# Row tiles of 32 in the tap matmuls, a filter sum by accumulating transfers, and a new order of work in a fused convolution and feed-forward kernel

## The chip, the cores and the metric

The kernel runs on one core of one Trainium2 chip. The metric is the device time of one launch in microseconds (us), as a median over runs. A profiled execution gives, beside it, a trace of every instruction on the five engines: PE (matmul), DVE (vector), ACT (scalar), POOL (GpSimd) and SP (which only issues transfers). Weight loads of the PE have a row of their own, PEld.

## The reference

The block is a gated long convolution followed by a feed-forward part, on 2048 tokens of width 640, all in bf16.

```
def reference(...):                       # S, D, F = 2048, 640, 1728
    x = A_q
    q = layernorm(x)
    k_shift = sum over t = 0..3 of  k delayed by (3-t) tokens * shift_k[:, 3-t]      # four taps per channel
    kv = k_shift * v
    y = irfft(rfft(kv, 2S) * rfft(ssm_k, 2S))[:S]  (bf16)  +  kv * ssm_D             # causal convolution over all tokens
    h = x + q * y
    n = layernorm(h)
    return h + (silu(n @ w_gate) * (n @ w_up)) @ w_down
```

## The kernel before

The 2048 tokens are cut into four blocks of 512, numbered 0 to 3. Within a block the tokens lie four to a partition (token 4p+j on partition p), so a tile of 512 x 640 is [128 partitions, 4, 640]. The convolution is done by odd-frequency transforms of length 512 per block: a filter spectrum for each of the four pieces of the filter (`kfwd`, tasks `kf0` to `kf3`), a signal spectrum for each block (`xfwd`, `xf0` to `xf3`), products of them on DVE (`prod(j, i)`, tasks `pji`, signal block j into output block i), and an inverse transform (`inverse`, tasks `ivi.j`, one for each of four token tiles of 128). After the inverse come the gating, the second layer norm and a transposing transfer into `hnT` (`hti.j`), and then the feed-forward part of that block (`ffn`): gate and up matmuls `fg` and `fu` in two halves of 256 tokens (a name such as `fg1.02` is block 1, half 0, third group), silu and copy out of PSUM on ACT (`sg`, `su`, `sv`), their product on DVE (`mu`), and the down matmuls `dn` (with `rs` for the residual sum, `ra` for an accumulating transfer of it into the token tile, and `out` for the store).

The filter spectra are combined (`kcomb`) so that C[m] holds the sum of the spectra m-1 and m: C[1] by two DVE additions (tasks `kc1.s0`, `kc1.s2`), C[2] by one DVE addition of 128 x 5120 elements (`kc2.s`, L687), C[3] by two accumulating transfers from POOL's queue (`kc3.0`, `kc3.1`; the lists `KS` and `KD` say which).

The taps (`taps`, tasks `tpi.c`) are matmuls. For a channel block c of 128 channels the four tap weights lie as diagonal matrices in `diag`; a matmul takes 64 channels (the rows), 128 columns of the shifted, transposed k as weights, and up to four diagonal pieces of 64 columns as the moving side. Seven shifts s = 0, 1, 2, 3, -1, -2, -3 need 4, 3, 2, 1, 3, 2, 1 such pieces. The two halves of 64 channels are two row tiles of the array and write to the two PSUM banks of one PSUM unit. A block has five channel blocks, taken as three tasks: `tpi.0` (two channel blocks), `tpi.2` (two), `tpi.4` (one); 70 matmuls in all. For blocks 1 to 3 (`KVACT`) an evacuation `ke` copies each task's result to SBUF, and DVE multiplies it with v (`kv`, L745). Block 0 multiplies straight from PSUM.

Nothing is scheduled at run time. `_Graph` records tasks with what they read and write; `PLAN` then lists by number, for each engine, the order of its tasks, and for each PSUM tile which of four units (two banks each) it lives in. Engines run their list strictly in order, and wait with semaphores where a task of another engine must be done. So a matmul task whose unit has not been evacuated stops the PE, whatever stands behind it. `fills` puts a few dummy matmuls before two of the first tasks.

The lines of the profile that matter below: L584, L602 and L622 are matmuls of the transforms, L734 the taps, L922 and L927 the inverse, L1032 gate and up, L1118 and L995 down; L458, L460 and L461 are evacuations (ACT, and DVE's two forms), L780 the products on DVE, L571 every accumulating transfer, L840 a small power on POOL in the layer norms, L453 the transposing transfers.

Of the kernel before, what the change touches and what calls it, by code (L numbers as in the profile page):

```python
# [50 lines left out]
class _Graph:  # L51
# [41 lines left out]
    def add(self, name, engs, fn, kind, r=(), w=(), pr=(), pw=(), skip=(), dma=False):  # L93
# [4 lines left out]
        t.opens = None  # L98
# [18 lines left out]
        for pt in pw:  # L117
            if not pt.writers:
                t.opens = pt
            else:  # L120
                t.deps.add(pt.writers[-1])
            pt.writers.append(t)
            pt.users.append(t)
            t.tiles.append(pt)
# [10 lines left out]
    def arrange(self, plan):  # L135
# [19 lines left out]
        for t in self.order["pe"]:  # L155
            if t.opens is not None:
                prev = last.get(t.opens.unit)
                if prev is not None:
                    t.pre = {x for x in prev.users if x.eng != "pe"}
                    t.deps.update(t.pre)  # L160
                last[t.opens.unit] = t.opens
# [21 lines left out]
    def emit(self, block):  # L183
# [29 lines left out]
        for t in self.glob:  # L213
            kn = known[t.eng]
            fill = self.fills.get(t.name)
            if fill:
                wait_for(t, t.pre | {x for x in t.deps if x.name == fill[0]})
                prog["pe"].append(lambda e, t=t, fill=fill: self.filler(e, t.opens, *fill))
# [50 lines left out]
    "act":  # L269
# [10 lines left out]
    "dve":  # L280
# [948 lines left out]
```

## Time and profile before

| | before |
|---|---|
| median of 3 runs | 258.16 us (257.98 to 258.31) |
| span of the profiled execution | 256.0 us |
| what lies around the span, against the median | 2.1 us |
| PE busy | 248.5 us, 97% |
| DVE busy | 199.8 us, 78% |
| ACT busy | 184.6 us, 72% |
| POOL busy | 58.6 us, 23% |

The profiled execution's time as such is not listed; its span is, and the difference to the median is taken as constant. In the views, busy times count an instruction from its start to its end; since matmuls overlap, an engine that is busy all the time may still have issued late, and the time between the starts of two matmuls says more than the busy share. A row of the timeline merges equal instructions: start, length, engine, line, and how many.

### The profile page before, as it was taken

To read this page: it belongs to the slowest core of one execution; us is meant where nothing else is said; L and a number is where in the kernel's file an instruction comes from. 1 tells how busy PE (TensorE), PEld (TensorE's weight loads), DVE (VectorE), ACT (ScalarE), POOL (GpSimd) and SP (SyncE) were. 2 spreads that over 40 slices of the span, in tenths; PEclk is the share of its full clock that TensorE was granted. 3 is DMA by queue.
4 is the path that set the end of the run, shared out by engine and by line. 5 is a ranking of instruction groups with operands and counts; after the bars stand their busy time and mean duration, and the time that the engine had idled before them with its cause. 6 is when DMAs were issued, how large, how long until landed. Compare 5 with 4: busy or idle time off the path is not lost.

```text
span 256.0 us, 5303 instructions
## 1 busy us (share of the span) xinstructions
PE 248.5 (97%) x2253; PEld 194.7 (76%) x2253; DVE 199.8 (78%) x256; ACT 184.6 (72%) x302; POOL 58.6 (23%) x56
## 2 busy tenths in 40 slices
PE   7999997999999999999999999999999999999995
PEld 4767773587888766888887766788886678888763
DVE  3698999999999999999999989999959534111142
ACT  2489999999996895587899789739981854526410
POOL 1001003082312053950030813334130314000000
PEclk9999999999999999999999999999999999999999
DMA  6999946787995049886956036497870142600011
GB/s 224 323 339 208 403 161 134 220 207 192 326 188 95 0 75 126 150 165 168 248 100 109 3 55 139 108 213 139 149 128 0 30 100 43 140 0 3 0 45 57
DMA packets 37620, 35.29 MB, mean 138 GB/s; under 512 B 21203, under 2 KB 32478, under 8 KB 37598
## 3 DMA queue, kind: packets, MB, share of 16 engines
q1 hardware_dynamic: 31792, 23.82, 33.2%
q0 software_dynamic: 5792, 11.14, 25.3%
q8 instruction: 17, 0.28, 0.4%
q14 instruction: 5, 0.04, 0.1%
q10 hardware_dynamic: 14, 0.01, 0.0%
HBM read 16.55 MB, written 2.62 MB: 75 GB/s over the span
## 4 chain that ended last, share of the span: by engine, by line
PE 59%; DVE 32%; DMA 4%; POOL 1%; SPq 1%; issue 1%; ACT 0%; DVEq 0%
PE ps L1032 32%; PE ps L1118 16%; DVE tt L780 9%; DVE Y L780 5%; DMA tab<-cst_tab 4%; PE ps L602 3%; PE ps L922 2%; DVE gu L1053 2%; DVE C L780 2%; DVE XH L637 2%; DVE C L564 2%; PE ps L995 2%; PE ps L622 2%; PE ps L584 2%; POOL mv L840 1%; SPq L450 1%
## 5 line engine op out<-in xcount | busy, mean ns | idle before, releaser
L1118 PE MATMUL ps<-Wd,gu 128*128 128x320 bf16 (+1 forms) x420 | 58.7, 300 | 0.0
L1118 PEld LDWEIGHTS ps<-Wd,gu 128*128 128x128 bf16 (+1 forms) x420 | 38.7, 97 | 18.4 <-issue 3.6
L780 DVE TENSOR_TENSOR tt<-XH,C 128x2560 bf16<-128x2560 bf16 (+1 forms) x31 | 47.8, 1572 | 0.6 <-ACT XH L458 0.6
L1053 DVE TENSOR_TENSOR gu<-gu,ub 128x1024 bf16<-128x1024 bf16 (+1 forms) x32 | 19.9, 621 | 26.4 <-ACT gu L1040 13.8
L1040 ACT ACTIVATE gu<-ps 128x1024 bf16<-128x1024 f32 (+1 forms) x32 | 29.4, 924 | 12.1 <-PE ps L1032 11.9
L1045 ACT ACTIVATE ub<-ps 128x1024 bf16<-128x1024 f32 x24 | 24.6, 1024 | 13.3 <-PE ps L1032 11.4
L1032 PE MATMUL ps<-hnT,GB 128*128 128x256 bf16 x280 | 34.0, 273 | 0.0
L1032 PE MATMUL ps<-hnT,UB 128*128 128x256 bf16 x280 | 33.8, 273 | 0.0
L1032 PEld LDWEIGHTS ps<-hnT,UB 128*128 128x128 bf16 x280 | 27.3, 98 | 3.4 <-ACT KO L458 0.2
L1032 PEld LDWEIGHTS ps<-hnT,GB 128*128 128x128 bf16 x280 | 27.2, 98 | 3.3
L1032 PE MATMUL ps<-hnT,GA 128*128 128x256 bf16 x240 | 28.8, 273 | 0.0
L1032 PE MATMUL ps<-hnT,UA 128*128 128x256 bf16 x240 | 28.5, 273 | 0.1
L840 POOL TENSOR_TENSOR mv<-mv,half 128x1 f32<-128x1 f32 x16 | 21.2, 1328 | 23.9 <-DVE mv L838 23.9
L1032 PEld LDWEIGHTS ps<-hnT,UA 128*128 128x128 bf16 x240 | 23.4, 98 | 3.4 <-ACT C L458 0.5
L1032 PEld LDWEIGHTS ps<-hnT,GA 128*128 128x128 bf16 x240 | 23.4, 98 | 3.2 <-DVE XH L461 0.3
L843 ACT ACTIVATE qo<-xh 128x640 bf16<-128x640 bf16 x28 | 21.0, 750 | 5.8 <-DMA xh<-in_A_q_dram 3.3
L584 PE MATMUL ps<-KT,tab 128*128 128x320 bf16 x128 | 19.8, 300 | 1.8 <-ACT K3r L458 0.7
L937 ACT ACTIVATE qo<-ps,one,st 128x640 bf16<-128x640 f32 x16 | 13.7, 887 | 9.8 <-PE ps L922 9.0
L571 POOL DMA_DIRECT2D xh<-RB x12 | 10.7, 889 | 34.4 <-DVE RB L1135 23.0
L584 PEld LDWEIGHTS ps<-KT,tab 128*128 128x128 bf16 x128 | 11.4, 98 | 8.6 <-ACT K3r L458 1.6
L840 POOL TENSOR_TENSOR st<-st,half 128x4 f32<-128x4 f32 x4 | 8.0, 1988 | 33.3 <-DVE st L835 21.5
L458 ACT ACTIVATE XH<-ps 128x640 bf16<-128x640 f32 x19 | 13.3, 736 | 1.4 <-PE ps L622 0.7
(112 smaller groups left out, 384.3 us busy)
## 6 DMA issues: line engine op xcount, KB each, us to landing
C<-US POOLq DMA_DIRECT2D x6, 640.0 KB, 6.0
kc<-in_A_ssm_k_dram SPq DMA_DIRECT2D x4, 640.0 KB, 10.3
xh<-in_A_q_dram SPq DMA_DIRECT2D x4, 640.0 KB, 5.6
out_dram<-xh SPq DMA_DIRECT2D x15, 160.0 KB, 1.9
kvo<-in_A_v_dram SPq DMA_DIRECT2D x3, 640.0 KB, 4.5
xh<-RB POOLq DMA_DIRECT2D x12, 160.0 KB, 2.9
Wd<-in_B_w_down_dram SPq DMA_DIRECT2D x1, 1280.0 KB, 7.9
C<-K3r POOLq DMA_DIRECT2D x2, 640.0 KB, 8.0
```

Source lines behind the costliest of these rows:

```text
L458: return e.activation(out=dst[1], in_=src(), func=ACTF.Copy, scale=scale)
L571: return g.add(name, "pool", lambda e, n: e.dma_start(dst, src, accum_op=ALU.add, max_dma_last_dim=4096), ("acc", 2 * int(np.prod(dst.shap ...
L584: last = e.matmul(pt.f(c, W), tab[:, f, cs, j], src[:, j, c * W:(c + 1) * W], start=(j == js[0]), stop=(j == js[1]))
L780: g.add(nm, "dve", lambda e, n_: e.tensor_tensor(out=d, in0=a, in1=b, op=op), ("sb", n * D), r=[a, b], w=[d])
L840: g.add(name + "r", "pool", lambda e, n: e.tensor_tensor(out=dst, in0=tmp, in1=hf, op=ALU.pow), ("pp", 4), r=[tmp, half[:]], w=[dst])
L843: g.add(name + "m", "act", lambda e, n: e.activation(out=junk, in_=x, func=ACTF.Identity, scale=-1.0 / D, accum_out=sm), ("aa", D, 0), r=[ ...
L937: g.add(nm + "e", "act", lambda e, n, pt=pt, q2=q2, s=s, j=j: e.activation(out=q2, in_=pt.f2(W), func=ACTF.Identity, scale=s[:, 3, j:j + 1 ...
L1032: last = e.matmul(pt.f(q // 2, 256, o=256 * (q % 2)), w[:, c, f0:f0 + P], hnT[:, c, cols], start=(c == 0), stop=(c == NC5 - 1))
L1040: g.add("sg%d.%d%d" % (i, h, gp), "act", lambda e, n, pa=pa, gv=gv, nf=nf: e.activation(out=gv, in_=pa.f(0, 256 * nf).rearrange("p (f x) - ...
L1045: g.add("su%d.%d%d" % (i, h, gp), "act", lambda e, n, pb=pb: e.activation(out=ub[:].rearrange("p b x -> p (b x)"), in_=pb.f(0, 1024), func ...
L1053: g.add("mu%d.%d%d" % (i, h, gp), "dve", lambda e, n, gv=gv, ubv=ubv: e.tensor_tensor(out=gv, in0=gv, in1=ubv, op=ALU.mult), ("sb", 256 * ...
L1118: last = e.matmul(pt.f(c, W), gu[k, fb, col(i, j)], Wd[k, fb, c * W:(c + 1) * W], start=st, stop=sp)
```

## The change

Three things are changed.

1. In `taps`, blocks 1 to 3 take channel blocks 0 to 3 as one task `tpi.0` with row tiles of 32 channels: four row tiles, four PSUM banks, that is two PSUM units opened by one task. A matmul now has 32 rows and 32 to 128 columns. Channel block 4 stays a task of its own with 64-row tiles (`tpi.4`). That makes 112 + 14 = 126 matmuls a block in place of 70. There are still three evacuations of the same sizes (`kei.0a`, `kei.0b`, `kei.4`), and two products with v in place of three. Block 0 is as before.
2. `KD = (2, 3)`: C[2] is made by two accumulating transfers from POOL's queue (`kc2.1`, `kc2.0`) and not by the addition on DVE.
3. `PLAN` is another: order on every engine and PSUM units. The recorder lets one task open several PSUM tiles. An option `DV` is added and is empty.

```diff
-    KD = (3,)
+    KD = (2,3)
     DD = (2,)
+    DV = ()
...
+    T32 = ((0, 4, 32), (4, 1, 64))
...
-            for c0 in (0, 2, 4):
-                nc_ = min(2, NC5 - c0)
-                pt = g.tile()
-
-                def mm(e, n, pt=pt, c0=c0, nc_=nc_):
+            for c0, nc_, rr in T32 if i in KVACT else ((0, 2, 64), (2, 2, 64), (4, 1, 64)):
+                nr = P // rr
+                pts = [g.tile() for _ in range(nr // 2)]
+
+                def mm(e, n, pts=pts, c0=c0, nc_=nc_, rr=rr, nr=nr):
                     for b in range(nc_):
                         c = c0 + b
                         for s in (0, 1, 2, 3, -1, -2, -3):
                             j0, j1 = max(0, s), min(3, 3 + s) + 1
                             k0 = 16 + s
-                            for r in range(2):
-                                rows = slice(64 * r, 64 * r + 64)
-                                last = e.matmul(pt.f(r, 64 * (j1 - j0), o=256 * b + 64 * j0), ks[rows, c, k0:k0 + 509:4], diag[rows, c, j0 - s:j1 - s, :],
-                                                start=(s == 0), stop=(s == -3))
+                            for r in range(nr):
+                                rows = slice(rr * r, rr * r + rr)
+                                x0 = rr * r % 64
+                                last = e.matmul(pts[r // 2].f(r % 2, rr * (j1 - j0), o=4 * rr * b + rr * j0), ks[rows, c, k0:k0 + 509:4],
+                                                diag[rows, c, j0 - s:j1 - s, x0:x0 + rr], start=(s == 0), stop=(s == -3),
+                                                **({"tile_position": (rr * r, 0)} if rr < 64 else {}))
                     return last
...
+                    for h, pt in enumerate(pts):
+                        kh_ = kr[:, 2 * h:2 * h + 2]
+                        evac("ke%d.%d%s" % (i, c0, "ab"[h] if nr > 2 else ""), (kh_, kh_),
+                             lambda pt=pt, nc_=nc_, rr=rr: pt.f2(4 * rr * nc_).rearrange("p r (b y) -> p r b y", b=nc_), 8 * rr * nc_, pt)
...
             if t.opens is not None:                       # in arrange: before
-                prev = last.get(t.opens.unit)
+            for pt in t.opens:                            # after: every tile that the task opens
+                prev = last.get(pt.unit)
```

The order, by the tasks' names, at the places that matter (a `|` stands where tasks are left out):

| place | before | after |
|---|---|---|
| PE, first transforms | kt0.0 kt0.1 xf0.01 xf0.00 kf0.011 kf0.100 | kt0.0 kt0.1 xf0.00 kf0.010 kf0.011 kf0.111 |
| PE, block 1 taps | kt3.0 kf1.110 tp1.2 tp1.0 iv0.0 iv0.1 tp1.4 | kt2.1 tp1.0 kf1.000 kt2.0 tp1.4 iv0.1 iv0.0 |
| PE, between the inverse of block 0 and the first gate | kf2, kf3 and xf1: 14 tasks, then fu0.00 | kf2, kt3.0, kf3 and xf1: 18 tasks, then fg0.00 |
| PE, block 1 | dn0.3 fu1.00 fg1.00 tp2.2 tp2.0 tp2.4 fg1.02 xf2.30 | tp2.4 dn0.1 dn0.2 dn0.3 fg1.00 fu1.00 fg1.01 tp2.0 fu1.01 fg1.02 xf2.20 |
| PE, block 1 to 2 | tp3.4 tp3.0 tp3.2 fg1.13 fu1.12 dn1.1 iv2.1 iv2.0 dn1.2 iv2.3 iv2.2 dn1.3, eight xf3, fg2.00 | tp3.0 dn1.1 tp3.4 dn1.2 iv2.0 iv2.1 dn1.3, three xf3, iv2.2, five xf3, iv2.3, fg2.00 |
| evacuations of the transforms on DVE up to block 1's products | kf0e.011 (and kte0.0) | xf0e.00 kf0e.000 kf1e.000 kf2e.001 xf1e.20 xf1e.00 kte3.0 |
| POOL, after the first layer norm | iv0.0r iv0.1r kb2.1 iv0.3r iv0.2r kb3.1 kc3.1 kc3.0 | iv0.1r lp0 iv0.0r kc2.1 kb2.1 iv0.3r iv0.2r kb3.1 kc2.0 kc3.1 kc3.0 |
| SP, block 1 | ht1.0 out0.0 ht1.1 | ht1.1 ht1.0 out0.0 |

More of the change, by code (lines that the diff above doesn't have):

```diff
@@ L97, in add @@
         t.pre = set()
-        t.opens = None
+        t.opens = []
         t.tiles = []
@@ L118, in add @@
             if not pt.writers:
-                t.opens = pt
+                t.opens.append(pt)
             else:
@@ L155, in arrange @@
         for t in self.order["pe"]:
-            if t.opens is not None:
-                prev = last.get(t.opens.unit)
+            for pt in t.opens:
+                prev = last.get(pt.unit)
                 if prev is not None:
-                    t.pre = {x for x in prev.users if x.eng != "pe"}
-                    t.deps.update(t.pre)
-                last[t.opens.unit] = t.opens
+                    t.pre |= {x for x in prev.users if x.eng != "pe"}
+                last[pt.unit] = pt
+            t.deps.update(t.pre)
         for t in self.tasks:
@@ L217, in emit @@
                 wait_for(t, t.pre | {x for x in t.deps if x.name == fill[0]})
-                prog["pe"].append(lambda e, t=t, fill=fill: self.filler(e, t.opens, *fill))
+                prog["pe"].append(lambda e, t=t, fill=fill: self.filler(e, t.opens[0], *fill))
             wait_for(t, t.deps)
@@ L731, in mm @@
                             k0 = 16 + s
[L732 to L738 removed]
+                            for r in range(nr):
[4 more added lines that the diff above has]
+                                                **({"tile_position": (rr * r, 0)} if rr < 64 else {}))
+                    return last
+                g.add("tp%d.%d" % (i, c0), "pe", mm, ("tap%d" % rr, nc_), r=[diag[:, c0:c0 + nc_], ks[:, c0:c0 + nc_, :]], pw=pts)
+                pt = pts[0]
                 cols = slice(c0 * P, (c0 + nc_) * P)
@@ L799, in prod @@
                 op2(nm + ".d", yim, u[:, :, 0], u[:, :, 1], ALU.add, 4)
+                return
+            if (j, i) in DV:
+                x, k, re = XH[j % 2][:], cm[:], tt[:, 1].rearrange("p a b d -> p (a b) d")
+                im = US[:].rearrange("p a b c d -> p (a b) c d")
+                ksw = bass.AP(k.tensor, k.offset + D, [list(k.ap[0]), [2 * D, 4], [-D, 2], [1, D]])
+                nm = "p%d%d" % (j, i)
+                for f2 in range(2):
+                    s = slice(f2, f2 + 3, 2)
+                    op2(nm + ".%da" % f2, t1, x[:, s], k[:, s], ALU.mult, 4)
+                    op2(nm + ".%dc" % f2, re[:, s], t1[:, :, odd], t1[:, :, 1 - odd], ALU.subtract, 2)
+                addto(nm + ".0e", y[:, :, odd], re)
+                op2(nm + ".0b", im, x, ksw, ALU.mult, 8)
+                for q in range(2):
+                    addto(nm + ".%df" % q, y[:, :, 1 - odd], im[:, :, q])
                 return
```

27 lines of the change are left out of this document (11 added, 16 removed), and 53 rows, old and new, of the table PLAN.

## The prediction

> **What bounds the kernel now.** I read first the chain that ended last, then the busy time by stages, then the timeline of PE at the seams between the stages. The stages show how full each engine is (after the length of the stretch: busy us and instructions of PE, PEld, DVE, ACT and POOL).
>
> ```profile
> 39.80:49.20 9.40, 7.35 (x44) 3.03 (x41) 9.02 (x12) 9.40 (x18) 2.38 (x2) 1.00 0.61 129
> 49.20:113.20 64.00, 63.58 (x588) 51.34 (x588) 63.40 (x69) 53.70 (x92) 26.44 (x19) 1.00 0.74 162
> 113.20:158.50 45.30, 45.27 (x425) 36.20 (x426) 43.73 (x55) 39.42 (x68) 11.17 (x9) 1.00 0.53 113
> 158.50:161.40 2.90, 2.66 (x18) 1.27 (x17) 2.63 (x5) 2.46 (x4) 1.47 (x2) 1.00 0.51 146
> 161.40:253.40 92.00, 91.97 (x780) 74.72 (x780) 48.69 (x72) 49.33 (x81) 15.17 (x17) 1.00 0.39 78
> ```
>
> PE is full from 49.2 on, but DVE is nearly full with it up to 158.5 (63.40 of 64.00, 43.73 of 45.30). So two engines are at their bound at once: less PE work pays in full only where DVE delivers in time. The chain gives the unit prices of PE.
>
> ```profile
> 14.72 3.96 PE ps L584 x28
> 113.95 2.18 PE ps L1032 x20
> 144.67 3.88 PE ps L1118 x28
> ```
>
> 20 matmuls of 256 columns in 2.18 us are 0.426 ns a column; 28 matmuls of 320 columns take 3.8 to 3.96 us, 0.136 us each. By this price the 44 matmuls of 39.80 to 49.20 need 6.0 us of the 9.40: PE stands still for 3.4 us there. It waits for evacuations (ACT is busy 9.40 of 9.40), and has no gate matmuls to fill in with before block 0's hnT lands. The other idle times of PE after 14.72 are small; I come to two of them. The last end is PE's, plus one residual sum and a store, which stay as they are.
>
> The profiled span is 256.0 us, the median 258.16: 2.1 us lie around the span and stay. 0.2% is 0.52 us, about what a measurement of this kernel can tell from no change.
>
> **The taps.** The rows of the three tap groups:
>
> ```profile
> 138.29 2.44 PE L734 MATMUL ps<-diag,kT 64*128 64x256 bf16 x70
> 140.67 0.50 PE L1032 MATMUL ps<-hnT,GB 128*128 128x256 bf16 x3
> 32.27 2.02 PE L734 MATMUL ps<-diag,kT 64*128 64x256 bf16 x56
> 34.23 2.35 PE L927 MATMUL ps<-OS,itab 128*128 128x320 bf16 x16
> 36.51 0.65 PE L734 MATMUL ps<-diag,kT 64*128 64x256 bf16 x14
> 37.09 0.72 PE L584 MATMUL ps<-KT,tab 128*128 128x320 bf16 x4
> L734 PEld LDWEIGHTS ps<-diag,kT 64*128 64x128 bf16 x280 | 10.0, 115 | 1.1 <-issue 0.7 <-DVE kT L460 0.2
> L734 PE MATMUL ps<-diag,kT 64*128 64x64 bf16 x80 | 7.6, 194 | 0.0
> ```
>
> A block's 70 matmuls hold PE from 138.29 to 140.67, 2.38 us. One row tile streams 1024 columns a channel block (16 pieces of 64), 5120 a block, 2.18 us at 0.426; both row tiles together would be 4.36. So the two tiles run side by side already, and 0.2 us are switching. From the first start to the last is 2.44 less the last one's 0.19, so 2.25 us: 2.15 of streaming and 0.10 for everything else. Of the 35 pairs ten have only 64 columns (27 ns), so two matmuls and two weight loads fit into 27 ns. The 280 weight loads of 115 ns sum to 32 us and keep PEld busy for 10.0: three are under way at a time, so those of different row tiles don't queue up.
>
> After: four channel blocks with four tiles side by side stream 4 x 512 columns, 0.87 us; the 8 sets of four with 32 columns (14 ns) I hold at the 27 ns that the shortest pair shows, +0.11. With 0.44 for the fifth channel block and 0.07 of small costs that is 1.5 us against 2.28 (2.38 less the leaving): 0.78 saved a block, 2.34 for three. A second excursion costs what block 1's split shows: 1.96 (32.27 to 34.23) plus 0.58 (36.51 to 37.09) against 2.38, 0.16. Blocks 2 and 3 are newly split: 0.32. Net -2.0 us on PE. The bounds: -2.3 without the floor of 27 ns; if each of the 126 matmuls cost the 33 ns that 70 take now, 4.1 us a block, +5.8 in all. I take -2.0, as the pairs are nearest to it.
>
> ACT's evacuations keep number and size. A unit more is held by one task: tp1.0 to tp3.0 must find two units free. In the new order their former owners are evacuated (kf1e, su1.00 with rs0.3, su1.12 with sg1.12) while at least one other PE task runs, so I cost that at nothing; uncovered, it would be one ACT evacuation, about 1 us.
>
> **The filter sum, and what DVE gets for it.**
>
> ```profile
> L687 DVE TENSOR_TENSOR C<-C,C 128x5120 bf16<-128x5120 bf16 x1 | 2.8, 2822 | 0.0
> L461 DVE TENSOR_SCALAR KO<-ps 128x640 bf16<-128x640 f32 x1 | 0.8, 825 | 0.4 <-PE ps L584 0.4
> L745 DVE TENSOR_TENSOR kvo<-XT,kvo 128x1024 bf16<-128x1024 bf16 x6 | 3.9, 685 | 0.0
> C<-K3r POOLq DMA_DIRECT2D x2, 640.0 KB, 8.0
> 53.43 5.21 POOL L840 TENSOR_TENSOR mv<-mv,half 128x1 f32<-128x1 f32 x1
> 27.47 0.71 ACT XH L458
> 83.16 1.40 DVE tt L780
> ```
>
> DVE loses 2.82 us, and 0.15 a block where two products with v become one. But the new order gives it five evacuations more between block 0's spectrum and block 1's products (kf1e.000, kf2e.001, xf1e.20, xf1e.00, kte3.0), 5 x 0.82 = 4.1. Net it has 1.1 us more in its fullest stretch. It starts that stretch about 0.5 earlier: the last evacuation of the signal spectrum starts at 27.47 now, behind two of kt2 on ACT; in the new order these come later, and PE has 12.0 us of work from 14.72 to that spectrum's end (6 x 0.54, 7 x 1.09, kt1 1.1), so it can start at about 26.9. 0.6 is left. The two transfers take 8.0 us to land and are first read by p02.d, in the old order at 83.16, in the new behind p11; kc2.0 goes out once kb2.1 has landed and behind kb3.1, by about 68, so lands by about 77: hidden. On POOL the issues stand before iv0.3r, where a power already took 5.21 us; iv0.3n is needed for the second half's hnT only, at least two gate tasks later.
>
> **The start.** The first matmul that needs the second half of the table waits until 14.72 in either order, since SP's first ten transfers are the same.
>
> ```profile
> 13.81 0.71 PE L584 MATMUL ps<-KT,tab 128*128 128x320 bf16 x4
> 14.72 1.52 PE L584 MATMUL ps<-KT,tab 128*128 128x320 bf16 x10 [0.20 <-DMA tab<-cst_tab]
> ```
>
> Before it the old order issues xf0.01, xf0.00 and kf0.011, 20 matmuls; the new one xf0.00, kf0.010 and kf0.011, 16. Four are left for later: +0.54. The fillers now stand behind wb4, which waits for its transfer, so the taps of block 0 come about 0.6 later; that fits into the 0.9 us between 13.81 and 14.72 as far as four fewer matmuls leave room.
>
> **The stall before the gates (39.8 to 49.2).** Two queues set when the first gate can start in the new order.
>
> ```profile
> 32.68 1.49 DVE OS L564
> 37.41 1.40 DVE C L684
> 38.81 0.40 DVE xh L944
> 39.47 0.72 ACT L843 ACTIVATE qo<-xh 128x640 bf16<-128x640 bf16 x1
> 43.12 0.71 ACT L458 ACTIVATE C<-ps 128x640 bf16<-128x640 f32 x1
> 48.96 0.81 ACT L458 ACTIVATE OS<-ps 128x640 bf16<-128x640 f32 x1
> hnT<-qo SPq DMA_TRANSPOSE x16, 2.6
> ```
>
> DVE: from the butterfly yb0.0 (now 32.7, then 32.2) to iv0.0n stand five operations of 1.40, the five evacuations (4.1), four small ones of 0.40 and kv (1.6): 14.3, so 46.5, and hnT lands 2.6 later, at 49.1. ACT: it starts iv0.1e at about 36, as now, and has then to xf1e.11 twelve evacuations (0.58 apart, ten steps from 43.12 to 48.96), seven operations of the norm (0.72 to 0.87) and ke1.4: 13.2, so 49.2. The first gate comes at about 49.3, against 49.2 now, with two transforms of xf1 and two of kf3 fewer left over (1.4 us). Of this gain of 1.3 the start (+0.54) and tp1 (-0.78) explain 0.24; about 1.0 is the stall's. Half of that I give back, since kf3.110 and kf3.010 stand behind the evacuations of the first gates: -0.5. Ends: 0 and -3.4.
>
> **Block 1.**
>
> ```profile
> PE ps L622 <- DVE kvo L745: 0.4, 1, 0.4
> ```
>
> PE waits once, 0.4 us, for kv at the first xf2 (near 113), which now stands behind mu1.00; the new order puts tp2.4 four tasks ahead and two more gate tasks before the first xf2. I take this wait as gone: -0.4.
>
> **Block 1 to 2.** Here cover is lost.
>
> ```profile
> 148.53 1.26 PE L922 MATMUL ps<-Y,itab 128*128 128x320 bf16 x8
> 149.62 3.94 PE L1118 MATMUL ps<-Wd,gu 128*128 128x320 bf16 x28
> 155.56 2.56 SPq L453 DMA_TRANSPOSE hnT<-qo  x2
> 161.32 0.94 PE L1032 MATMUL ps<-hnT,GA 128*128 128x256 bf16 x7
> ```
>
> From the first inverse of block 2 (148.53) to the first gate (161.32) PE has two down tasks (7.7), four inverses (2.2) and eight xf3 (2.2), 12.1 of 12.8 us. The hnT of the first two tiles is issued until 158.1 and has landed at about 159.5: a chain of 11.0. In the new order dn1.2 comes before the inverses, so only 8.2 us of work lie there. The chain gets shorter by what DVE no longer does in its midst (an evacuation of 0.82), 10.2. PE then waits 2.0 in place of 0.7: +1.3. The bounds are +0.6 (a chain of 9.6, as for the first tile alone) and +2.1 (11.0).
>
> Block 2 to 3 has the same loss of cover, one part of a down task (8 x 0.136 = 1.1), but DVE idles there and the present order has that much in hand. 0.
>
> Sum: +0.54 -2.0 -0.5 -0.4 +1.3 = -1.06, so 258.16 - 1.06 = **257.1 us**.
>
> **Rivals.** *ACT relieved, the stall goes.* ACT is full (9.40 of 9.40) in the stretch in which PE stands still, and five of its evacuations go to DVE. If that rather than hnT sets the stretch, half of the 2.9 us that I keep goes too: 257.1 - 1.5 = 255.6. Against it: DVE is busy 9.02 of 9.40 there.
>
> *DVE late, slower.* Place: the hnT of block 1's first half. Its second transfer is issued behind a store:
>
> ```profile
> 100.20 0.36 SPq L1147 DMA_DIRECT2D out_dram<-xh  x1
> 100.61 1.21 SPq L453 DMA_TRANSPOSE hnT<-qo  x1
> 103.59 1.15 PE L1032 MATMUL ps<-hnT,UA 128*128 128x256 bf16 x9
> ```
>
> It lands at 103.2, and PE wants it at 103.59. The new order puts both transfers ahead of the store, which gives about a microsecond; DVE's 0.6 fits in. If DVE is later by over a microsecond, the first gate of block 1 waits, and what PE has saved so far is lost: block 1's taps (0.8), the 0.5 of the stall and the 0.4 at 113.2 are not gained, and 0.7 more is waited: 257.1 + 2.4 = 259.5.
>
> *The row tiles give little.* If a set of four costs two pairs (54 ns at least), the four channel blocks take 1.51, a block 2.0: 0.3 saved and not 0.78, so 257.1 + 1.4 = 258.5. If every matmul holds the array for 27 ns, the 112 take 3.05, a block 3.5, +1.2 a block: 257.1 + 2.3 + 3.7 = 263.1. Against the latter speak the pairs: 35 of them leave 0.10 us over streaming, and ten of 64 columns would need 0.27. [...]
>
> **How the numbers follow.** The forecast, 256.4 to 258.0: 0.40, of which 0.28 lie below 257.64 and 0.12 within 0.52 of 258.16. The stall goes: 0.24. DVE late: 0.28. Row tiles give little: 0.08, a quarter of it within 0.52. That makes faster 0.52, same 0.14, slower 0.34. The range leaves out the worst of the row tiles' case and the ends of the others: 255.2 (the stall mostly gone) to 259.9 (DVE a little later still).
>
> **What would show it.** L734 with 126 matmuls a block and about 1.0 us for the 112; PE at 20 matmuls of 320 columns or fewer before the wait for tab; the first L1032 at 49 to 50 with ACT full before it; no wait of L622 near 113; 2 us of idle before block 2's first gate; DVE busy as long as before. Wrong it would be if the 112 took over 1.5 us, if the first gate came before 48.5, or if L1032 waited for hnT near 104.

## The result and the profile after

| | before | after |
|---|---|---|
| median | 258.24 us (257.98 to 259.72, 4 runs) | 261.57 us (261.36 to 262.09, 4 runs) |
| ratio, 95% interval | | 1.0117 [1.008, 1.0154] |
| span of the profiled execution | 256.0 us | 259.8 us |
| PE busy, PE idle in the span | 248.5, 7.5 us | 246.6, 13.2 us |

The changed kernel is 1.2% slower, 3.3 us by the medians and 3.8 by the two profiled spans; 257.1 was forecast. PE has 1.9 us less to do, as forecast, and stands still 5.7 us longer. The busy times by stages say where (length of the stretch, then PE, PEld, DVE, ACT, POOL). The second to fourth rows run from the first gate of a block to the first gate of the next, blocks 0, 1 and 2. After:

```profile
39.80:49.20 9.40, 8.18 (x63) 5.11 (x62) 9.40 (x13) 9.40 (x19) 1.88 (x4) 1.00 0.95 257
49.67:106.42 56.75, 53.93 (x464) 42.84 (x463) 54.01 (x61) 46.56 (x82) 24.41 (x17) 1.00 0.73 141
106.42:165.11 58.69, 55.47 (x668) 43.83 (x669) 55.92 (x65) 48.19 (x79) 14.01 (x14) 1.00 0.71 131
165.11:212.22 47.11, 47.11 (x400) 38.31 (x401) 35.57 (x51) 34.19 (x60) 12.96 (x13) 1.00 0.56 110
```

The same stretches of blocks 0 and 1 before:

```profile
49.23:103.59 54.36, 54.36 (x458) 43.30 (x459) 53.76 (x59) 46.56 (x82) 18.53 (x13) 1.00 0.71 160
103.59:161.32 57.73, 57.07 (x572) 45.44 (x570) 55.90 (x70) 48.91 (x81) 20.47 (x16) 1.00 0.60 124
```

The first gate comes 0.4 later than before. Block 0's stretch is 2.4 longer, with PE's work 0.4 less; block 1's is 1.0 longer, with PE's work 1.6 less. DVE's work is the same to 0.3 us in both. Behind that nothing changes. PE's waits after (us, times, longest):

```profile
PE ps L1048 <- DMA hnT<-qo: 2.9, 2, 2.0
PE ps L943 <- ACT qo L953: 1.9, 1, 1.9
PE ps L938 <- ACT OS L454: 0.6, 1, 0.6
```

L1048 is gate and up (L1032 before). So both losses sit in front of a first gate. The chain that ended last leads into them (start, length, engine, line); first block 1's:

```profile
80.92 1.40 DVE tt L782
82.32 0.09 DVE st L854
82.49 7.56 POOL st L856
90.13 0.88 ACT qo L953
...
102.06 0.19 DVE tt L782
102.25 4.13 DMA hnT<-qo
106.42 1.59 PE ps L1048 x13
...
143.42 1.23 PE ps L731 x99
148.53 0.57 PE ps L731 x14
...
161.11 3.91 DMA hnT<-qo
165.11 0.93 PE ps L1048 x7
```

The task at 82.49 is `la1r`, a power of 128 x 4 elements on POOL, which took 1.40 us in the kernel before:

```profile
77.51 1.40 POOL L840 TENSOR_TENSOR st<-st,half 128x4 f32<-128x4 f32 x1 [1.60 <-DVE st L838]
```

ACT evacuates block 1's inverse (L953) only with its result, at 90.13 (84.89 before); PE's next inverse has no free PSUM unit meanwhile and waits 1.9, and hnT arrives 0.9 after the last down task, by a transfer that took 4.13 us (2.60 before). DVE's next instruction behind p02.a, the gate product of that inverse, waits for the same evacuation:

```profile
91.05 0.49 DVE L960 TENSOR_TENSOR xh<-xh,qo 128x640 bf16<-128x640 bf16 x1 [1.91 <-ACT qo L953]
```

So the pause of DVE in which the power ended is itself an effect of the hold: DVE had come to the first thing that needs the power's result. The chain's last rows are block 2's gate, behind a transfer of hnT of 3.91 us.

### The profile page after: what moved, and what is told of

Same layout as the page of the kernel before. It is cut to its first block, busy times and chain, and to the rows that moved or that the text cites. A ratio compares the mean times of both kernels' runs of the same rounds, so it can differ in the third digit from the quotient of the medians.

```text
span 259.8 us, 5625 instructions
## 1 busy us (share of the span) xinstructions
PE 246.6 (95%) x2421; PEld 193.7 (75%) x2421; DVE 196.8 (76%) x251; ACT 186.0 (72%) x303; POOL 59.8 (23%) x58
## 4 chain that ended last, share of the span: by engine, by line
PE 59%; DVE 26%; ACT 6%; DMA 4%; POOL 3%; issue 1%; ACTq 0%
PE ps L1048 34%; PE ps L1134 15%; DVE tt L782 8%; DVE Y L782 4%; DMA hnT<-qo 3%; POOL st L856 3%; ACT qo L953 2%; DVE C L560 2%; PE ps L731 2%; PE ps L580 2%; DVE XH L633 2%; PE ps L1011 2%; ACT qo L861 1%; PE ps L938 1%; ACT qo L859 1%; DVE gu L1069 1%
## 5 line engine op out<-in xcount | busy, mean ns | idle before, releaser
L1048 PE MATMUL ps<-hnT,UB 128*128 128x256 bf16 x280 | 34.0, 273 | 0.0
L1048 PE MATMUL ps<-hnT,GB 128*128 128x256 bf16 x280 | 34.0, 273 | 0.0
L1056 ACT ACTIVATE gu<-ps 128x1024 bf16<-128x1024 f32 (+1 forms) x32 | 28.5, 914 | 5.7 <-PE ps L1048 5.4
L1048 PE MATMUL ps<-hnT,GA 128*128 128x256 bf16 x240 | 28.7, 273 | 2.9 <-DMA hnT<-qo 2.9
L1048 PEld LDWEIGHTS ps<-hnT,GB 128*128 128x128 bf16 x280 | 27.4, 98 | 3.3
L1048 PEld LDWEIGHTS ps<-hnT,UB 128*128 128x128 bf16 x280 | 27.4, 98 | 3.2
L1048 PE MATMUL ps<-hnT,UA 128*128 128x256 bf16 x240 | 28.8, 273 | 0.0
L1048 PEld LDWEIGHTS ps<-hnT,GA 128*128 128x128 bf16 x240 | 23.2, 98 | 6.6 <-ACT qo L861 2.3
L856 POOL TENSOR_TENSOR mv<-mv,half 128x1 f32<-128x1 f32 x16 | 15.1, 948 | 51.3 <-DVE mv L854 50.2
L1048 PEld LDWEIGHTS ps<-hnT,UA 128*128 128x128 bf16 x240 | 23.3, 98 | 2.8
L856 POOL TENSOR_TENSOR st<-st,half 128x4 f32<-128x4 f32 x4 | 13.6, 3397 | 29.4 <-DVE st L851 21.3
L580 PE MATMUL ps<-KT,tab 128*128 128x320 bf16 x128 | 19.2, 299 | 1.2 <-ACT KO L454 1.2
L567 POOL DMA_DIRECT2D xh<-RB x12 | 10.7, 892 | 39.6 <-ACT RB L1150 33.2
L953 ACT ACTIVATE qo<-ps,one,st 128x640 bf16<-128x640 f32 x16 | 14.0, 889 | 7.7 <-PE ps L938 3.8
L580 PEld LDWEIGHTS ps<-KT,tab 128*128 128x128 bf16 x128 | 12.2, 98 | 6.5 <-ACT KO L454 1.9
L1150 ACT ACTIVATE RB<-ps,st 128x640 bf16<-128x640 f32 x10 | 7.9, 791 | 8.6 <-DMA xh<-RB 5.9
```

The lines of the kernel that those rows point to most:

```text
L567: return g.add(name, "pool", lambda e, n: e.dma_start(dst, src, accum_op=ALU.add, max_dma_last_dim=4096), ("acc", 2 * int(np.prod(dst.shap ...
L580: last = e.matmul(pt.f(c, W), tab[:, f, cs, j], src[:, j, c * W:(c + 1) * W], start=(j == js[0]), stop=(j == js[1]))
L856: g.add(name + "r", "pool", lambda e, n: e.tensor_tensor(out=dst, in0=tmp, in1=hf, op=ALU.pow), ("pp", 4), r=[tmp, half[:]], w=[dst])
L953: g.add(nm + "e", "act", lambda e, n, pt=pt, q2=q2, s=s, j=j: e.activation(out=q2, in_=pt.f2(W), func=ACTF.Identity, scale=s[:, 3, j:j + 1 ...
L1048: last = e.matmul(pt.f(q // 2, 256, o=256 * (q % 2)), w[:, c, f0:f0 + P], hnT[:, c, cols], start=(c == 0), stop=(c == NC5 - 1))
L1056: g.add("sg%d.%d%d" % (i, h, gp), "act", lambda e, n, pa=pa, gv=gv, nf=nf: e.activation(out=gv, in_=pa.f(0, 256 * nf).rearrange("p (f x) - ...
```

## Experiments

Line numbers in the kernels of the first four experiments with moved instructions are 26 to 32 lower; the code is the same. Orders are shown by task names, since the lists hold numbers only.

**The power that is held, block 1.** First the changed kernel once more, unaltered.

> The changed kernel unaltered, for a second profile beside the first, since three of its first four executions had a shorter span (259.1 to 259.4 for 259.8) at a mean granted clock of 0.993. Theory 'the hold of la1r differs from run to run, and a PE idle of 2 us costs clock': la1r ends near 87 in place of 90.04 when DVE leaves a gap of a tenth of a microsecond before mu0.12, the first gate of block 1 comes at about 104 and not 106.4; the first gate of block 2 still waits 2 us, and behind that wait TensorE's granted clock stands at 0.5 for some 3 us, which gives back 1.7 us. Rival: la1r takes 7.5 us in every execution and the clock stays at 1.0. The time is 261.6 in either case.

262.31 us, ratio 1.0118 [1.0067, 1.0168]. POOL's row for `la1r`:

```profile
82.37 4.21 POOL L856 TENSOR_TENSOR st<-st,half 128x4 f32<-128x4 f32 x1 [3.62 <-DVE st L854]
```

The same instruction in the same order took 4.21 us, not 7.56. It ended 0.9 after the end of yb1.1, behind which DVE began mu0.12 some 0.07 late; in the first profile it ended 0.9 after the end of p02.a, the next place where DVE paused. The clock stayed at 1.0 here, so that half of the expectation did not show; in three of the kernel's first four executions the mean granted clock was 0.993. The first gate of block 1 still waited, 1.8 us, now for the second hnT transpose alone, which took 5.4 us (2.6 before).

Then `la1v`, which opens the power, moved up:

```diff
 dve: ... p11.1d p11.1c
+     la1v
      mu0.03 p11.1e mu0.10 p02.d
-     la1v
      yb1.0 mu0.11 yb1.1 mu0.12 p02.a ...
```

> The changed kernel with one instruction moved: DVE's small la1v (L854), which opens the power la1r of block 1's first layer norm, stands ahead of mu0.03 (near 78.6 us) and not behind p02.d (82.24). In the changed kernel la1r then held POOL from 82.49 to 90.04, 7.55 us, and ended 0.9 after the end of p02.a, the last of five DVE operations that stood back to back. Theory 'POOL is held off by DVE': la1r is over before 81, ACT evacuates iv1.1 at about 87.0 and not at 90.13 (la1.3x ends 86.31, the inverse 86.94), PE's wait of 1.9 at 89.2 goes; DVE takes iv1.1's gate product right behind p02.a, at 89.1 and not at 91.05, so hnT lands 1.9 earlier, at 104.5, and the first gate of block 1 comes then: -1.9 us, 259.7 median. Rival 'DVE is late by its work' (the prediction's own): the first gate stays within 0.5 of 106.4 and the time within 0.5 of 261.6. Rival 'la1r is slow by itself': it takes over 5 us again wherever it starts; a gain of under 1 us.

Three rounds gave 261.49 us, ratio 1.0133 [1.0093, 1.0172], no gain. `la1r` took 1.14 us, the inverse was evacuated at 86.66, PE's wait of 1.9 was gone and the first gate of block 1 came at 103.56, better than expected; then the gate of block 2 waited 2.05 and the clock dipped. Five rounds of the same kernel:

> The first experiment again (the changed kernel, la1v ahead of mu0.03), with five rounds. In its profile the first gate of block 1 came 2.9 us earlier and the first gate of block 2 as well, and the clock dip behind the latter gave 1.65 back; in time it was within its interval of the changed kernel. Theory 'la1r is a loss that the clock dip masks': 0.3 to 1.2 us faster than the changed kernel, 260.4 to 261.3. Rival 'no gain at all, the wait in front of block 2 takes it': 261.6 or more.

260.28 us, ratio 1.0062 [1.0026, 1.0098]. So the move is worth half a per cent by this measurement and nothing by the first; the two barely overlap, and part of that spread is the clock (below). In this second profile `la1r` took 1.11 us, and the first gate of block 1 still waited:

```profile
104.43 2.36 PE L1048 MATMUL ps<-hnT,GA 128*128 128x256 bf16 x20 [2.01 <-DMA hnT<-qo]
```

It waited for the second of two hnT transposes, issued at 98.78 and landed at 104.39, 5.6 later. In all the profiles with the new orders this transfer took 3.9 to 5.6 us, in the kernel before 2.6. There POOL's `xh<-RB` (160 KB) goes out 0.3 ahead of it (0.7 behind it before), and a store and a load of v (640 KB) follow it on SP. So a transfer is slowed at this gate too; which of the others slows it was not tried.

The control is the kernel before with this one instruction late:

```diff
 dve: ... p11.1c
-     la1v
      mu0.02 p11.1e mu0.03 yb1.0 mu0.10 yb1.1 p02.d
+     la1v
      p02.a iv1.0g ...
```

> The kernel before with la1v alone moved late, behind p02.d, as the changed kernel has it; nothing else of the change. Theory 'POOL is held off by DVE': la1r starts near 84.7 with p02.a (2.8 us) behind it on DVE, ends near 88.2 in place of 78.91, 0.9 after p02.a; iv1.0 is evacuated at 88.2 and not 84.89, its gate product comes at 89.1 and not 87.22; the first gate of block 1 moves from 103.6 to 105.1 to 105.5: +1.5 to +1.9 us, 259.7 to 260.1. If the place of la1v doesn't matter: within 0.5 of the kernel before, 258.2.

261.29 us, ratio 1.0129 [1.0091, 1.0167]: more than expected. POOL's row and PE's longest wait:

```profile
84.55 3.53 POOL L808 TENSOR_TENSOR st<-st,half 128x4 f32<-128x4 f32 x1 [8.95 <-DVE st L806]
```

```profile
PE ps L895 <- ACT qo L905: 2.7, 1, 2.7
```

It ended at 88.08, 0.9 after p02.a (87.18), as expected; what was not expected is a granted clock of 0.79 from 88 to 92 behind PE's wait. Three of its four executions had a mean clock of 0.993; the one at 1.0 took 260.15 us, 2.2 over the kernel before. Together with the dip, one misplaced 0.16 us instruction reproduces the size of the whole loss in the old kernel.

**The transfer beside hnT, block 2.** POOL's and SP's queues of the changed kernel in front of that gate:

```profile
154.18 0.91 POOL L567 DMA_DIRECT2D xh<-RB  x1 [0.68 <-ACT RB L1150]
154.78 1.54 POOL L567 DMA_DIRECT2D C<-US  x1
...
158.66 3.74 SPq L449 DMA_TRANSPOSE hnT<-qo  x2
```

`C<-US` is p13.1e, 640 KB; in the trace it lands at 162.4. Issuing the two transposes beside it took 3.74 us (2.56 before), and the first landed 5.0 after its start (3.2 before). In the kernel before p13.1e went out at 129; the new order on POOL has it behind `la2r` and `ra1.2`.

```diff
 pool: ... p12.1e p13.0e
+      p13.1e
       ra1.0 ra1.1 la2r ra1.2
-      p13.1e
       iv2.0r ...
```

> The changed kernel with one transfer moved on POOL's queue: p13.1e (640 KB, accumulating, L567) right behind p13.0e, as in the kernel before, and not behind la2r and ra1.2. In the changed kernel it ran from 154.78 to 162.41, and SP's first hnT transpose of block 2 beside it took 2.41 us to issue and landed 4.96 after its start (1.24 and 3.23 before); the first gate of block 2 waited 2.0 for it. Theory 'collision of transfers': p13.1e goes out at about 133.3, the two transposes take 1.2 each and land near 161.5 and 162.9, the first gate of block 2 comes some 2 us earlier, 163.1 for 165.1: -1.9 us, 259.7. Rival 'lost cover alone' (the prediction's +1.3 at this place): the wait of 2.0 stays and the time is within 0.5 of 261.6.

259.59 us, ratio 1.0079 [1.0035, 1.0123], against 1.0117 for the changed kernel: 1.0 us by the ratios, 1.7 by the distance of the medians to the kernel before; the two intervals overlap. The wait of 2.0 at the gate is gone, only 1.3 us at the inverses ahead of it stay; but 1.6 came up at a later gate. With both moves:

> The changed kernel with both moves: la1v ahead of mu0.03, p13.1e behind p13.0e. If the two losses are independent, the sum of the two gains: -1.9 - 1.9 = -3.8, 257.8, about even with the kernel before. If what is gained at block 1 is lost again in front of block 2 (DVE sets the pace between them), it is no better than the better of the two, 259.7.

259.28 us, ratio 1.0038 [0.9998, 1.0077]; five rounds to narrow it:

> Both moves again (la1v ahead of mu0.03, p13.1e behind p13.0e), with five rounds. Theory 'these two places make most of the loss': 258.8 to 259.6, 0.2 to 0.5% behind the kernel before. Rival 'the sum of many new seams': 260 or more, over 0.7% behind.

259.66 us, 1.0038 [1.001, 1.0066]. SP and PE's waits in that run:

```profile
156.36 2.71 SPq L449 DMA_TRANSPOSE hnT<-qo  x2
```

```profile
PE ps L1048 <- ACT qo L859: 1.2, 1, 1.2
PE ps L938 <- ACT OS L454: 0.6, 1, 0.6
PE ps L731 <- ACT RB L1150: 0.6, 1, 0.6
PE ps L1048 <- DMA hnT<-qo: 0.4, 1, 0.4
```

Two moved instructions take back 0.8 of the 1.2%. Of the waits left, the largest (1.2 here, 1.3 in the three rounds) stands at the gate of block 2's second half; the view names ACT as its releaser. ACT's su2.01 was moved for it:

```diff
 act: ... sg2.01
+     su2.01
      la3.1s la3.2m
-     su2.01
      la3.2s ...
```

> The changed kernel with la1v ahead of mu0.03, p13.1e behind p13.0e, and on ACT su2.01 moved ahead of la3.1s and la3.2m, right behind sg2.01. With the first two moves alone PE waited 1.31 us in block 2's FFN (176.24 to 177.55) for su2.01, which stood on ACT behind la3.2m, and that waited for DVE's la3.1x. Theory 'what was repaired is given back at the next order': su2.01 runs at 174.1, the wait goes, and the time falls by 1.3 us against the two moves alone, 258.0, even with the kernel before. Rival: the wait only moves on, to a later gate of block 2; no change against the two moves alone (259.3).

260.14 us, 1.0082 [1.0058, 1.0106]: no gain, and the wait stayed at that gate with 1.8 us, though su2.01 was over at 175.2 and the gate began at 178.09. So the theory took the releaser that the view of waits names, an ACT task, for the cause. The queues of POOL and SP in this run show another:

```profile
170.26 1.21 POOL L567 DMA_DIRECT2D XH<-OS  x1
```

```profile
168.46 5.05 SPq L449 DMA_TRANSPOSE hnT<-qo  x2
```

`XH<-OS` is xb3.4, again 640 KB. The second of the two transposes, ht2.3, was issued from 170.81, beside it, and landed at 178.00, 7.2 later (2.6 before, where xb3.4 went out behind both). The gate of block 2's second half, which needs it, began at 178.09. In all three runs with both moves, in the one with p13.1e alone and in the second run of the changed kernel it begins 0.09 behind that landing; in the first profile the landing (179.19) was just in time for the later PE (179.84). So this is the same collision at a second place, and its 1.2 to 1.8 us are of the size of what the two moves leave. Moving xb3.4 was not tried.

**The clock.** In the first run with `la1v` early the stretches around block 2's gate were (the third figure from the end, 1.00 and then 0.62, is the granted clock):

```profile
160.20:162.24 2.04, 0.00 (x0) 0.03 (x1) 2.03 (x4) 2.01 (x6) 0.22 (x1) 1.00 1.16 241
162.24:163.24 1.00, 1.00 (x6) 0.75 (x7) 0.97 (x2) 0.86 (x2) 0.84 (x1) 0.62 0.76 275
163.24:165.24 2.00, 2.00 (x12) 1.35 (x10) 2.00 (x4) 1.25 (x3) 0.00 (x0) 0.50 0.43 76
165.24:166.24 1.00, 1.00 (x8) 0.77 (x7) 1.00 (x2) 0.50 (x2) 0.00 (x0) 0.68 0.60 225
```

PE stood still for 2.04 us; then the clock was at half for about 3.4, in which PE does 1.7 us less by these figures (0.38, 1.00 and 0.32). To take away the idle time and not the wait, matmuls that nobody reads were put into it:

```diff
     "k0t4.0": ["zmem", 1],
+    "fg2.00": ["xf3e.00", 7],
```

> The changed kernel with la1v moved up (as in the first experiment) and, in addition, seven matmuls of 512 columns that nobody reads, put on PE behind ACT's xf3e.00 and ahead of block 2's first gate, where PE otherwise stands still for 2.05 us (160.20 to 162.24). They compute nothing that is used and take away no wait. In the first experiment the granted clock fell to 0.5 from about 162.7 to 165.6, so that the first gate task took 4.0 us and not 2.35. Theory 'an idle of over 2 us costs clock': with PE busy in the wait the clock stays at 1.0, and the time falls by 1.6 us against the first experiment (261.49 there). Rival 'the clock dips for another reason' (the load, the place in the program): the dip stays and the time is the same, or longer by what the seven matmuls take over the wait (0.2).

No run of ten had a mean clock below 0.999; of the 16 runs without the matmuls seven had 0.987 to 0.993. After the filled wait:

```profile
161.02:163.12 2.10, 1.58 (x8) 0.64 (x10) 2.08 (x4) 2.07 (x6) 0.28 (x1) 1.00 1.13 258
163.12:168.00 4.88, 4.88 (x46) 4.37 (x45) 4.85 (x9) 2.98 (x7) 0.79 (x1) 1.00 0.60 199
```

So here the idle time did cost the clock. The median, 260.19 us, ratio 1.0073 [1.0039, 1.0107], is 1.3 below the first run with `la1v` early, but equal to its five rounds: a dip comes in fewer than half of the executions, so it widens the spread more than it moves the median. Not every such wait leads to one: in these profiles a dip followed idle times of 1.7, 2.05, 2.7 and 2.7 us, and none followed 2.0, 2.0, 2.0, 2.1 and 2.7. All four dips were of about one length: the mean granted clock of the two stretches of 4 us that hold each was, in this order, 0.64 and 0.94, 0.81 and 0.76, 0.79 and 0.78, 0.63 and 0.94. That lacks 1.68 to 1.72 us of full clock, as 3.4 us at 0.50 do. So the length of the idle time alone does not tell whether a dip follows; what else decides, these runs do not show. For the idle times of 2.1 and 2.7 without a dip no record of the clock was kept; there the spacing of the matmuls behind them shows the full clock (20 in 2.42 us of PE's work and 20 in 2.64, where the dip behind an equal wait of 2.7 has 18 in 3.81).

**The taps alone.** The old orders with the new taps: `tpi.0` and `tpi.2` become one task at the later one's place, in the same two units.

```diff
 pe: ... fu1.00 fg1.00
-    tp2.2 tp2.0 tp2.4
+    tp2.0 tp2.4          (blocks 1 and 3 alike)
     fg1.02 ...
```

> The kernel before, its orders kept, with the taps of the change alone: the two tap tasks of two channel blocks each become one of four channel blocks with 32-row tiles at the place of the later of the two, and their two products with v become one. Theory 'the taps pay as predicted': PE's busy time falls by about 0.6 a block, 1.9 in all; block 1's share (0.7) lies ahead of the stall at 40 to 49 and is lost there, block 3 gives 0.5 back as tp3.0 now waits for sg1.12 (139.27): -0.6 to -1.2, 257.0 to 257.6. Rival 'DVE sets the pace': PE's busy time falls by 1.9 and the time stays within 0.3 of 258.2. Rival 'row tiles give little': PE's busy time falls by less than 1.

258.09 us, 0.9978 [0.994, 1.0017]. With five rounds:

> The kernel before with the 32-row taps alone, once more, five rounds. Theory 'the taps gain what DVE leaves of them': 0.2 to 0.4% faster than the kernel before, 257.2 to 257.7. Rival 'DVE sets the pace, PE's 1.1 us turn into waits': within 0.2%, 257.7 to 258.7.

258.14 us, 0.9998 [0.9972, 1.0024]: in the old orders the taps gain nothing that stands out of the noise, at most 0.3%. PE's busy time fell by 1.1, and new waits took it: 0.6 at the gate behind block 2's taps, whose evacuations now both start after the whole task, and 0.8 around block 3's. Taking these away:

```diff
 pe:  fu1.00 fg1.00 tp2.0
-     tp2.4 fg1.02 xf2.30 xf2.31 fg1.01
+     fg1.02 tp2.4 fg1.01 xf2.30 xf2.31     (units 0 and 2 exchanged from here on)
 act: la2.2x
+     sg1.12
      la2.3m
-     sg1.12
      rs1.0 ...    (and rs0.3 ahead of sg1.02, ke2.4 behind it)
```

> The kernel before with the 32-row taps alone, and three places around them mended: in block 2 fg1.02 and fg1.01 stand ahead of and behind tp2.4, so that fg1.02 takes the unit that sg1.00 empties (109.27) and not the one that ke2.0a empties (110.59), with rs0.3 and ke2.4 moved on ACT to match; in block 3 ACT's sg1.12, which tp3.0 waits for, stands ahead of la2.3m. In the run with the taps alone PE waited 0.63 at 110.0, 0.18 at 113.0 and 0.41 and 0.40 at 139 to 141. Theory 'the taps are worth what they save where nothing else waits': these 1.6 us go, blocks 2 and 3 keep 1.0 to 1.2 of it: 257.0, 1.1 us faster than the kernel before. Rival 'DVE sets the pace in front of block 2' (55.9 of 57.7 us busy there): the waits move to the first gate of block 2, and the time stays within 0.3 of the run with the taps alone (258.1).

259.16 us, 1.002 [0.9979, 1.0061]. The waits moved to other gates of the same stretch (1.16 us at 143.6), and in its profile the old order's `la1r`, untouched, was held:

```profile
77.64 10.68 POOL L856 TENSOR_TENSOR st<-st,half 128x4 f32<-128x4 f32 x1 [1.71 <-DVE st L854]
```

It was 1.40 us in the profile of the taps alone, and 10.68 in another execution of that same kernel. So the old order is open to the hold too, by chance. Two last runs take the chance out: DVE's instruction behind `la1v` waits for `la1r`.

```diff
+    "holds": {"la1": 1},
     "fills": {
```

> The kernel before with the 32-row taps alone, and with one wait added: DVE's mu0.02, the instruction behind la1v, waits for POOL's la1r. Theory 'la1r is held off only while DVE works': it takes 1.0 to 1.2 us in this and every run (1.05 beside an idle DVE, the third block's la3r), DVE loses 1.2 us, which block 1's hnT has in hand (landed 102.3, wanted at 103.7); no run has PE's wait of 2.7 us at 87 nor the clock dip behind it; the median is that of the better runs with the taps alone, 257.3 to 257.9. Rival 'DVE's 1.2 us are on the path': 258.5 to 259.3.

> As the run before it, with the three places around the taps mended too (fg1.02 and fg1.01 around tp2.4 with their units, rs0.3 and ke2.4 on ACT; sg1.12 ahead of la2.3m). Theory 'the taps are worth what they save where nothing else waits': the waits at 110 and 139 to 141 are gone, 0.5 to 1.0 us faster than the other: 256.6 to 257.2. Rival 'DVE sets the pace in front of block 2': no faster than the other, the waits stand at other gates of block 1's FFN.

259.08 us, 1.0052 [1.0032, 1.0072], and 259.9 us, 1.0073 [1.0048, 1.0099]. POOL's row in the first of them, and PE's longest wait:

```profile
77.26 1.03 POOL L856 TENSOR_TENSOR st<-st,half 128x4 f32<-128x4 f32 x1 [2.69 <-DVE st L854]
```

```profile
PE ps L1048 <- ACT XT L454: 1.7, 1, 1.7
```

With DVE idle the power takes 1.03 us, as expected. But the 1.16 us that DVE stands still for it cost 0.5%, 1.4 us against the taps alone: both rivals hold. DVE, not PE, sets the pace of these stretches, and a saving of PE's there is returned as a wait.

**The transfers alone.** In the old orders `kc2.s` on DVE is replaced, first with kc2.1 ahead of kb2.1 on POOL, then with both transfers behind kb3.1 and `la1r` ahead of kc3.0, without and with the taps:

```diff
 dve:  xb1.5
-      kc2.s
       kb3.0 ...
 pool: iv0.1r
+      kc2.1                                 (first version)
       kb2.1 iv0.3r iv0.2r kb3.1
+      kc2.1 kc2.0                           (second version; the first has kc2.0 only)
       kc3.1 ...
```

> The kernel before, its orders kept, with the accumulating transfers for the third filter spectrum alone: kc2.s (2.82 us on DVE) becomes kc2.1 ahead of kb2.1 and kc2.0 behind kb3.1 on POOL's queue. The prediction held the transfers for hidden and had the waits at 113.2 (0.4) depend on DVE: -0.4, 257.8, at most -1.0 if the stretch in front of block 1 gets shorter too. Rival 'POOL pays for it': the two issues (1.2 to 1.7 us each on POOL) hold up iv0.3r and la1r, or the transfers slow others: +0.3 or more.

> As the run of the transfers alone, with the better places: kb3.1, kc2.1, kc2.0, kc3.1, la1r, kc3.0 on POOL; the taps as before. Theory 'the place of kc2.1 cost it' (it held kb2.1 by 6 us, and through ACT's kf3e.111 PE by 1.4 us; kc3.0's wait held la1r): PE's wait of 1.42 at 63.6 goes, kb2.1 lands near 58 again, la1r is over by 79, the time is that of the kernel before or 0.4 less: 257.8 to 258.3. Rival 'the transfers themselves slow the others wherever they stand': again 0.6% slower, 259.8, with PE waiting for a landing somewhere else.

> The kernel before, its orders kept, with both parts of the change: the 32-row taps at the old places, and the transfers for the third filter spectrum, now placed behind kb3.1 on POOL's queue (kb3.1, kc2.1, kc2.0, kc3.1), with la1r ahead of kc3.0. So kb2.1 is not behind kc2.1 (in the run of the transfers alone it landed at 64.1 in place of 58.2, and ACT's kf3e.111 waited for it), and la1r isn't behind the wait of kc3.0. Theory 'the parts pay, the new orders don't': with DVE relieved by 2.8 us the waits that the taps' saving ran into get shorter; PE works 1.9 less: 257.2, about -1.0 us. Rival 'the parts pay nothing even in the old orders, since other engines set the pace': within 0.5 of 258.2.

260.46 us, 1.0061 [1.0027, 1.0095]; 261.31 us, 1.0133 [1.01, 1.0167]; 260.84 us, 1.0114 [1.0089, 1.0138]. All slower. In the first, kc2.1 held back kb2.1's landing from 58.2 to 64.1, and ACT waited for that:

```profile
64.21 1.90 ACT L454 ACTIVATE KO<-ps 128x640 bf16<-128x640 f32 x3 [1.44 <-DMA C<-KO]
```

In the other two this wait is gone, as the theory had it, and a larger one came. DVE in the run with the taps:

```profile
DVE Y L782 <- DMA C<-K3r: 3.1, 1, 3.1
```

The instruction is p02.a: it writes over C[2], and kc3.0 must have read that. Two transfers more in the chain of 640 KB transfers made kc3.0 land at 86.67 (80.76 before), so DVE was given 2.8 us of work less and waited 3.1. The last run takes the transfers out of the changed kernel:

```diff
 pool: iv0.2r
-      kc2.1
       kb2.1 ... kb3.1
-      kc2.0
       kc3.1 ...
 dve:  xb1.4
+      kc2.s
       kb3.0 ...
```

> The changed kernel with the third filter spectrum's sum back on DVE: kc2.1 and kc2.0 leave POOL's queue, kc2.s (2.82 us) stands ahead of kb3.0 on DVE; all else as in the changed kernel. In the old orders the transfers cost 0.6 to 1.3%: they lengthened the chain of 640 KB transfers on POOL's queue whose last, kc3.0, must have read C2 before p02.a may write there, and DVE stood still 3 to 4 us at p02.a. In the changed kernel kc3.0 lands at 83.12, p02.a starts at 86.31. Theory 'here the transfers pay, as they start at 48.6': without them DVE is 2.8 later from 64 on, block 1's hnT is late by as much: +2 to +2.8, 263.6 to 264.4. Rival 'the transfers are worth nothing here either': within 0.6 of 261.6.

265.16 us, ratio 1.0238 [1.0192, 1.0283]: in the new orders, where kc2.1 goes out at 48.6 and kc3.0 lands 3.2 us before p02.a, the transfers are worth 1.2%, and the new orders without them cost 2.4%. PE's waits there, with DVE 2.5 later at `la1v` and `la1r` held for 7.55 us again:

```profile
PE ps L1048 <- DMA hnT<-qo: 2.4, 2, 1.7
PE ps L1048 <- ACT gu L1056: 2.2, 2, 1.5
PE ps L943 <- ACT qo L953: 2.1, 1, 2.1
```

No version of this study beats the kernel before; the taps alone equal it.

## Why the prediction was wrong

The forecast was -1.06 us; the profiled spans give +3.8. Of these 4.9 us, 2.8 stand in front of block 1's first gate, 1.7 in front of block 2's, and 0.4 in front of block 0's.

*The start, +0.54:* the reason given did not hold. The second half of the table landed at 13.04 (14.59 before), so nothing waited for it; but block 0's taps began 1.4 later, and by 14.72 PE had begun 11 of the matmuls with the table (16 forecast, 20 before). Nine fewer are 1.2 us at 0.136 each. That the first gate came near the forecast all the same (49.67 for 49.3; 49.23 before) is in part luck.

*The taps, -2.0:* right as work, wrong as time. The 112 matmuls took 1.23 us against 1.0 forecast, with the fifth channel block 1.80 a block in place of 2.38; PE's busy time fell by 1.94. This is the first step that failed: the sum takes PE's saving in full, though its own first table shows DVE busy 63.40 of 64.00 us. In the old orders it was worth 0.0% (0.9972 to 1.0024); in the changed kernel the saving is there as work, and the waits of the two terms below outweigh it. The 27 ns a matmul of the worst rival, 3.05 us for the 112, did not show: with four row tiles side by side they took 1.23 us, 11 ns each.

*The stall, -0.5:* about right. PE's work in 39.80 to 49.20 rose from 7.35 to 8.18, 0.8.

*Block 1's wait for kv, -0.4:* right; no such wait is left near 113.

*Block 1 to 2, +1.3:* the 2 us of idle time before the gate came, but not for the reason given. With p13.1e out of the way the gate doesn't wait and 1.3 us stand at the inverses instead, which is the lost cover; the 2.0 are a collision on top. The prediction followed SP's queue there and left out POOL's, on which p13.1e had moved behind `la2r`. What was mis-sized is the term: 3.0 us of idle time more (3.2 against 0.2) where 1.3 was forecast.

*DVE's 1.1 us more and the powers on POOL, 0:* the second step that failed, and the largest. DVE was late by about what was forecast: p02.a ended 1.8 later, of which 1.2 are two products (`mu0.11`, `mu0.12`) that now stand ahead of it, so 0.6 is left. But the prediction costed POOL's powers at nothing, though it quoted one of 5.21 us, and looked only at whether the result of *that* one was urgent. `la1r`'s is, for ACT's evacuation of block 1's inverse, and its opener was moved in front of five DVE operations without a pause. In the profiled execution PE stood still for 2.8 us up to the first gate of block 1: 1.9 at the inverse, and 0.9 at the gate, for the hnT that was issued late and took 4.1. With `la1v` early the gate came 2.9 earlier. In the other profile of the same kernel the power took 4.2 and the wait at the inverse was absent, so this cost differs from execution to execution.

*The transfers hidden:* right here (kc2.0 landed at 75.7, read at 80.8), but only as the new orders send them early. The bound that the prediction did not see is the other end of the chain: when kc3.0 lets p02.a go.

*Rivals.* "DVE late" had the right place, block 1's hnT, and the right sign, with a price of 259.5 against 261.6 and a mechanism that the runs refute: DVE's work is the same to 0.3 us, and with `la1v` early, at the same work of DVE, the gate came at 103.56. "The stall goes" did not come, and "row tiles give little" neither.

## What to carry to other kernels

Where two engines are full, a saving on one is worth what the other leaves of it: price it at the engine that sets the pace. Here a us of DVE cost about 1.1 to 1.2 us of time where it was added (1.4 for a wait of 1.16, 3.1 by the ratios for the sum of 2.82), and PE's saving gave nothing clear of noise; taking the sum off DVE in the old orders gained nothing either, since the longer chain of transfers then held ACT (1.44 us) or DVE (3.1). In a new static order, check every small instruction on the path whose engine can be held off by another one (here 1.03 to 10.68 us for one power), and every queue for large transfers that have moved beside small urgent ones (here 3.74 us to issue two transposes, 2.56 before). A releaser named by a view of waits is a guess where it had long been done: look at the landing of the transfers first.

## What the hardware showed

*One power on POOL was held off by a whole row of DVE instructions.* This power of 128 x 4 elements took 1.03 us beside an idle DVE and 1.1 to 10.7 beside a busy one, and it ended 0.9 after the end of the DVE instruction behind which it got in. In the cases of 3.5 us and more DVE paused behind that instruction, for 0.07 to 1.9 us; in those of 1.1 to 1.4 no pause can be seen in the trace. Equal neighbours gave 1.40 and 10.68 us in two executions of one kernel; what decides between the two stays open. Five DVE instructions in a row went ahead in the changed kernel (7.55 us), eight in the longest case (10.68). Two single-element powers took 0.54 and 0.55 us beside DVE instructions that read PSUM (after, at 41.15 and 44.07 us).

*Behind an idle PE the granted clock fell to 0.50 for 3.4 us, in some executions.* It did so behind idle times of 1.7, 2.05, 2.7 and 2.7 us, and not behind 2.0, 2.0, 2.0, 2.1 and 2.7. With matmuls in the wait of 2.05 no run of ten had a mean clock below 0.999, without them seven of 16 had 0.987 to 0.993. What decides between a dip and none stays open.
